# From the MLP's second tile on: all engines in the order of the text, weight sums spread over the second tile

## Chip, cores and metric

The kernel runs on one core of a Trainium2 chip. The metric is device time in microseconds (us) of one execution. A core has five engines with queues of their own: PE (TensorE, matmuls; PEld are its weight loads), DVE (VectorE), ACT (ScalarE), POOL (GpSimd) and SP (SyncE, which here issues nearly all DMAs). An engine works off its queue in order, and semaphores tie the queues together.

## The reference

Attention with a bias made of cumulative sums, then a Fourier mixing, then a normalised MLP with a residual:

```python
attn = softmax(causal(scale * q @ k.T + min(bias, 0))) @ v      # 8 batches, 8 heads, 576 x 64
x = attn.transpose(0, 2, 1, 3).reshape(8, 576, 512)
u = x + real(fft(fft(x, axis=1), axis=2))
un = (u - mean(u)) / sqrt(var(u) + 1e-6)
out = u + relu(un @ w_ch1) @ w_ch2                              # 512 -> 2048 -> 512
```

`w_ch1` and `w_ch2` come in double precision and are rounded to single in the kernel. Most matmul operands are split into a high part of fewer bits and a low remainder, and three matmuls replace one: high by high, low by high, high by low.

## The kernel before

Attention and Fourier mixing take about the first 680 us and leave `u` in DRAM, transposed: 512 channels in four blocks of 128 partitions, 4608 tokens along the free dimension. The MLP then runs over nine tiles of 512 tokens. The hidden dimension of 2048 is cut into 16 slices `f` of 128.

The first tile (`first_tile`, plain matmuls) shares its time with the end of the mixing and with the conversion of the weights out of double precision (`load_w`, `rounded`). The first layer's weights stay on chip as pairs (`wh`, `wl`). The second layer's go to DRAM (`wD`, line 120) and come back in each tile.

From the second tile on (`fast_tile`) two slices make a pair `g`, eight pairs in a tile. A pair's first layer is a 2 x 2 block product done with seven block products instead of eight (Strassen's scheme): seven products `k` of six matmuls each (line 338), whose results ACT and DVE combine in `cs` (lines 342 to 350), then relu on ACT (line 330, high part `zh`) and its remainder on DVE (line 331, `zl`). Three of the seven left operands are sums of weight blocks, made once by `sums_w(g)` (`sh`, `sl`: lines 144 to 164). The right operands are seven blocks of the tile's normalised tokens, four of them sums (`combine`, lines 230 to 233), split by `block` (lines 221 and 222).

Behind each product the text puts one or two groups of the second layer for the pair before: three matmuls (lines 249 to 251) into one of four accumulators. The weights of a slice's second layer are loaded by SP, cast on ACT, and the remainder is taken on POOL (`load_w2`, lines 127 to 129; four buffers). Both loads, casts and subtractions stand at the head of a pair; they are used in the pair after. When the last slice's group for a quarter `j` is through, in pair 0 of the next tile, `done(j)` multiplies the accumulator by the inverse deviation (DVE, line 276), adds `u` (POOL, line 277; `w`, fetched by line 275) and stores (SP, line 278). `o` and `w` have two buffers each.

Meanwhile `side(g, k)` prepares the next tile: `ln_tile` loads `u` (line 187), sums it (189 to 191), spreads the mean by a matmul with ones (68, 69, 177, 178), subtracts it (197), squares on ACT and adds on POOL in turn (200 to 203), takes the root and the reciprocal (208, 209); then `combine` and the blocks.

What sets the order: the text is traced once, and a planner with a cost model of its own orders each engine's queue. `tc.manual_schedule(engines={PE})` takes PE out of this from the second tile on: PE follows the order of the text, the other four are planned. The planner is free to draw later steps forward where it sees an engine idle.

Of the kernel before, what the change touches and what calls it, by code (L numbers as in the profile page):

```python
# [40 lines left out]
def fused_kernel(ctx, tc, qkT, vA, sP, wP, tabD, tabS, corr, out):  # L41
# [81 lines left out]
    def load_w2(f):  # L123

        h = w2p.tile([128, 512], F32R, tag="w2h", name="w2h", bufs=4)
        low = w2p.tile([128, 512], F32R, tag="w2l", name="w2l", bufs=4)
        nc.sync.dma_start(out=low.bitcast(F32), in_=wD[f, :, 512:1024])
        nc.scalar.copy(h, low.bitcast(F32))  # L128
        nc.gpsimd.tensor_sub(low, low.bitcast(F32), h.bitcast(F32))  # L129
        W2[f] = (h, low)  # L130

    def sums_w(g):

        (ah, al), (ch, cl) = W[2 * g], W[2 * g + 1]
        sh = sp.tile([128, 768], F32R, tag=f"sh{g}", name=f"sh{g}")
        sl = sp.tile([128, 768], F32R, tag=f"sl{g}", name=f"sl{g}")

        def tmp():
            return sx.tile([128, 256], F32, tag="sx", name="sx", bufs=5)

        def whole(h, low, x):
            t = tmp()
# [4 lines left out]
        def parts(t, h, low):  # L147
            nc.scalar.copy(h, t)
            nc.vector.tensor_sub(low, t, h.bitcast(F32))  # L149
# [5 lines left out]
        parts(a22, ch[:, 0:256], cl[:, 0:256])  # L155
        a11 = whole(ah, al, 0)
        s2 = tmp()
        nc.vector.tensor_sub(s2, a22, a11)
        parts(s2, sh[:, 0:256], sl[:, 0:256])
        yield 1.0  # L160
        nc.vector.tensor_sub(a21, a11, a21)
        parts(a21, sh[:, 256:512], sl[:, 256:512])
        a12 = whole(ah, al, 1)
        nc.vector.tensor_sub(a12, a12, s2)
        parts(a12, sh[:, 512:768], sl[:, 512:768])
        yield 1.0
        SW[g] = (sh, sl)

    W, W2, SW = {}, {}, {}

    def spread_sum(t, name):
# [3 lines left out]
        split(th, tl, t)  # L175
        m = bank(name)
        nc.tensor.matmul(m, ones, th, start=True, stop=False)
        nc.tensor.matmul(m, ones, tl, start=False, stop=True)
        return m

    def ltmp(name):
# [2 lines left out]
    def ln_tile(t0, lag):  # L184

        u = lnp.tile([128, 4, TOK], F32, tag="u", name="u")
        (nc.sync if t0 else nc.scalar).dma_start(out=u, in_=uD[:, :, t0:t0 + TOK].rearrange("c p t -> p c t"))
        t, t2 = ltmp("t"), ltmp("t2")
        nc.gpsimd.tensor_add(t, u[:, 0], u[:, 1])  # L189
        nc.vector.tensor_add(t2, u[:, 2], u[:, 3])  # L190
        nc.vector.tensor_add(t, t, t2)  # L191
        yield lag
        pm = spread_sum(t, "mu")
        mu = ltmp("mu")
        nc.scalar.copy(mu, pm)
        for j in range(4):
            nc.vector.tensor_sub(u[:, j], u[:, j], mu)
            yield 0.5
        t, t2 = ltmp("t"), ltmp("t2")
        nc.scalar.activation(t, u[:, 0], AF.Square)  # L200
        for j in range(1, 4):
            nc.scalar.activation(t2, u[:, j], AF.Square)
            nc.gpsimd.tensor_add(t, t, t2)  # L203
            yield 0.7
        yield lag
        pv = spread_sum(t, "var")
        r = lnp.tile([128, TOK], F32, tag="r", name="r", bufs=2)
        nc.scalar.activation(r, pv, AF.Sqrt, bias=eps)
        nc.vector.reciprocal(r, r)
        LN[t0] = (u, r)  # L210

    LN, BL = {}, {}

# [3 lines left out]
    def block(t0, k, src):  # L217

        h = bp.tile([128, 2, 256], F32R, tag="bh", name="bh", bufs=9)
        low = bp.tile([128, 2, 256], F32R, tag="bl", name="bl", bufs=9)  # L220
        nc.scalar.copy(h, src)
        nc.vector.tensor_sub(low, src, h.bitcast(F32))  # L222
        BL.setdefault(t0, {})[k] = (h, low)

    def combine(t0):
# [4 lines left out]
        nc.gpsimd.tensor_sub(t3, b22, b12)  # L230
        nc.vector.tensor_sub(b12, b12, b11)
        nc.vector.tensor_sub(t2, b22, b12)
        nc.vector.tensor_sub(t4, b21, t2)
        return [b11, b21, t2, b12, t3, b22, t4]

    held = []

# [20 lines left out]
    def accs():  # L258
        return [accp.tile([128, TOK], F32, tag=f"acc{j}", name=f"acc{j}") for j in range(4)]

    def writer(t0, acc, r):
        last = t0 + TOK == NT
        whole = []

        def done(j):
            if last and not whole:
                w = lnp.tile([128, 4, TOK], F32, tag="u", name="u")
                nc.sync.dma_start(out=w, in_=uD[:, :, t0:t0 + TOK].rearrange("c p t -> p c t"))
                whole.append(w)
            o = op.tile([128, TOK], F32, tag="o", name="o", bufs=2)  # L270
            if last:
                w = whole[0][:, j]
            else:
                w = op.tile([128, TOK], F32, tag="w", name="w", bufs=2)
                nc.sync.dma_start(out=w, in_=uD[j, :, t0:t0 + TOK])
            nc.vector.tensor_mul(o, r, acc[j])
            (nc.vector if last else nc.gpsimd).tensor_add(o, o, w)
            (nc.scalar if last and j % 2 else nc.sync).dma_start(out=out[j, :, t0:t0 + TOK], in_=o)

        return done  # L280

    def first_tile(t0):
        _, r = LN[t0]
        acc = accs()
        done = writer(t0, acc, r)
        bl = BL.pop(t0)
        load_w2(0)
        for f in range(NF):
            while min(f + 2, NF) not in W and next(feed, None) is not None:
                pass  # L290
            if f + 1 < NF:
                load_w2(f + 1)
            wh, wl = W[f]
            h = bank("h")
            for k in range(2):
                i = 0
                for a, b in ((wh, 0), (wl, 0), (wh, 1)):
                    for j in range(4):
                        nc.tensor.matmul(h[:, 256 * k:256 * k + 256], a[:, j * 128:(j + 1) * 128], bl[j // 2, k][b][:, j % 2], start=i == 0, stop=i == 11)
                        i += 1  # L300
            zh = zp.tile([128, TOK], F32R, tag="zh", name="zh", bufs=3)
            zl = zp.tile([128, TOK], F32R, tag="zl", name="zl", bufs=3)
            nc.scalar.activation(zh, h, AF.Relu)
            nc.vector.scalar_tensor_tensor(out=zl, in0=h, scalar=0.0, in1=zh.bitcast(F32), op0=ALU.max, op1=ALU.subtract)  # L304
            for g in groups():
                g()
            held.append((acc, zh, zl, f, done))
            yield 1.0

    def fast_tile(t0, side):  # L310
        _, r = LN[t0]
        bl = BL.pop(t0)
        acc = done = None
        for g in range(NF // 2):
            load_w2(2 * g)
            load_w2(2 * g + 1)
            todo = groups()
            n = len(todo)
            (ah, al), (ch, cl) = W[2 * g], W[2 * g + 1]
# [13 lines left out]
            for k, (p, start) in enumerate(((b1, True), (b2, True), (b1, False), (b3, True), (b1, False), (b3, False), (b1, False))):  # L333
# [22 lines left out]
                    relu(z[1], lo, p)  # L356
                for x in range(n * k // 7, n * (k + 1) // 7):
                    todo[x]()
                side(g, k)
            if g == 0:  # L360
                acc = accs()
                done = writer(t0, acc, r)
            held.extend((acc, z[x][0], z[x][1], 2 * g + x, done) for x in range(2))


# [361 lines left out]
    def plain(t0):  # L727
        for i in range(2):
            for k in range(2):
                block(t0, (i, k), quarter(LN[t0][0], i, k))  # L730
                yield 1.0

    stage_ctx = ExitStack()
# [89 lines left out]
    feed = rest()  # L823

    def early(t0):
        blocks.extend(combine(t0))
        for k in range(5):
            block(t0, k, blocks[k])
            yield 1.0

    blocks = []
    weave([first_tile(tiles[0]), NF], [chain(idle(1000), mixing), FOURIER * 0.6], [ahead(), 100],
          [later(chain(ln_tile(tiles[1], 1), early(tiles[1])), 4), 16])
    for _ in feed:
        pass
    for k in range(5, 7):
        block(tiles[1], k, blocks[k])
    for g in range(2):
        weave([sums_w(g), 1.0])
    order.enter_context(tc.manual_schedule(engines={mybir.EngineType.PE}))  # L840
    for x, t0 in enumerate(tiles[1:], 1):
        coming = tiles[x + 1] if x + 1 < len(tiles) else None
        norm = ln_tile(coming, 1) if coming is not None else iter(())
        blocks = []

        def side(g, k):
            if x == 1 and k % 2 == 0 and g + 2 < NF // 2:
                if k == 0:
                    adding[0] = sums_w(g + 2)
                next(adding[0], None)  # L850
            if coming is None:
                return
            if 1 <= g <= 5 and k % 3 == 2:
                next(norm, None)
            if g == 5 and k == 6:
                for _ in norm:
                    pass
                blocks.extend(combine(coming))
            if g == 6 and k in (2, 5):
                block(coming, k // 3, blocks[k // 3])  # L860
            if g == 7 and k < 5:
                block(coming, k + 2, blocks[k + 2])

        adding = [None]
        fast_tile(t0, side)
    for call_ in groups():
        call_()
    order.close()
# [138 lines left out]
```

## Time and profile before

| | us |
|---|---|
| median of 3 runs (1507.11 to 1510.95) | 1507.59 |
| the profiled execution | 1506.13 |
| its span, first to last instruction | 1504.4 |
| PE busy (88% of the span) | 1331.1 |
| DVE busy (61%) | 916.7 |
| ACT busy (48%) | 717.4 |
| POOL busy (46%) | 690.6 |

In rows of the timeline the columns are start and duration in us, engine, line of the kernel, operation, output<-inputs, shape and count; in brackets stands how long the engine sat idle before it and whose end released it. In the chain of work they are start, duration and what ran. In tables by stage, each engine's busy time and instruction count follow the stretch and its length; then come the granted TensorE clock, the share of DMA time and GB/s. A busy PE is not a PE at its peak, because matmuls overlap; the distance from one matmul's start to the next is the measure.

### The profile page before, as it was taken

What the parts mean: (1) busy time and instruction counts of PE and PEld (TensorE: products, weight loads), DVE (VectorE), ACT (ScalarE), POOL (GpSimd) and SP (SyncE); (2) the same over time, 40 slices, a digit from 0 to 9 for tenths busy, and PEclk for the clock granted to TensorE, in tenths of its full rate; (3) what the DMA queues carried; (4) which work ended last, traced back from release to release, by engine and by line L of the source; (5) the groups of instructions that cost most, each with busy time, mean ns of one, the idle gap of its engine ahead of it and who ended that gap; (6) DMA issues with size and microseconds to landing.
All of it is one profiled execution on the core that took longest, in us unless ns stands there. A gap on an engine that the chain in (4) does not pass through costs nothing.

```text
span 1504.4 us, 22206 instructions
## 1 busy us (share of the span) xinstructions
PE 1331.1 (88%) x7534; PEld 1126.7 (75%) x7534; DVE 916.7 (61%) x2034; ACT 717.4 (48%) x1641; POOL 690.6 (46%) x644
## 2 busy tenths in 40 slices
PE   4988979889898987777759999999999999999998
PEld 2766857677686766666548888888788888888897
DVE  6677677677767676969894453545536354453423
ACT  3776656666565653334434443434434344443432
POOL 6454546464546464655573252433425234252321
PEclk9998989999899988898879999999999999999999
DMA  8555655556555553424431231412313132231311
GB/s 212 155 156 156 153 152 137 165 140 176 159 160 152 135 157 123 137 75 149 141 126 56 77 100 49 134 49 71 105 50 127 50 109 67 66 110 50 120 50 56
DMA packets 106941, 173.50 MB, mean 115 GB/s; under 512 B 14408, under 2 KB 41897, under 8 KB 106827
## 3 DMA queue, kind: packets, MB, share of 16 engines
q1 hardware_dynamic: 104379, 168.08, 38.2%
q0 software_dynamic: 1632, 2.43, 0.8%
q10 hardware_dynamic: 816, 1.57, 0.3%
q8 instruction: 59, 0.97, 0.3%
q14 instruction: 55, 0.45, 0.1%
HBM read 122.39 MB, written 25.69 MB: 98 GB/s over the span
## 4 chain that ended last, share of the span: by engine, by line
PE 35%; DVE 5%; DMA 4%; POOL 4%; ACT 2%; issue 2%; SPq 0%; POOLq 0%; ACTq 0%; DVEq 0%
PE b L338 17%; PE acc L249 6%; PE acc L250 6%; PE acc L251 6%; DMA u<-uD 2%; POOL t L203 2%; DMA w2l<-wD 2%; POOL w2l L129 1%; DVE t L191 1%; POOL t L189 1%; ACT w2h L128 1%; DVE sl L149 0%; DVE bl L222 0%; DVE we L86 0%; DVE wm L84 0%
## 5 line engine op out<-in xcount | busy, mean ns | idle before, releaser
L129 POOL TENSOR_TENSOR w2l<-w2l,w2h 128x512 fp32r<-128x512 f32 x144 | 190.1, 1321 | 385.1 <-ACT w2h L128 334.1
L249 PE MATMUL acc<-zh,w2h 128*128 128x512 f32 x576 | 232.6, 404 | 19.5 <-ACT w2h L128 19.4
L250 PE MATMUL acc<-zh,w2l 128*128 128x512 f32 x576 | 232.8, 404 | 3.0 <-POOL w2l L129 2.9
L251 PE MATMUL acc<-zl,w2h 128*128 128x512 f32 x576 | 230.8, 401 | 4.0 <-DVE zl L304 4.0
L671 PE MATMUL pavB<-P,va 128*128 128x320 f32 (+2 forms) x640 | 199.2, 400 | 6.9 <-ACT stage L675 6.2
L643 ACT ACTIVATE P<-ps 128x320 f32<-128x320 f32 (+4 forms) x384 | 144.7, 391 | 114.7 <-PE ps L640 110.3
L607 PE MATMUL pm<-KQ 128*128 128x256 f32 (+4 forms) x384 | 158.1, 430 | 39.3 <-DVE Mx L614 19.3
L614 DVE CUSTOM_DVE_ANT_0 trash<-pm,amask 128x128 bf16<-128x128 f32 (+3 forms) x256 | 123.6, 483 | 79.3 <-PE pm L607 62.7
L639 PE MATMUL ps<-KQ 128*128 128x256 f32 (+3 forms) x384 | 152.7, 401 | 19.0 <-ACT P L643 12.2
L330 ACT ACTIVATE zh<-cs 128x256 fp32r<-128x256 f32 (+1 forms) x128 | 67.2, 525 | 162.0 <-DVE cs L350 98.6
L128 ACT CAST w2h<-w2l 128x512 fp32r<-128x512 f32 x144 | 88.8, 617 | 103.6 <-DMA w2l<-wD 103.1
L251 PEld LDWEIGHTS acc<-zl,w2h 128*128 128x128 f32 x576 | 110.9, 192 | 31.7 <-DVE zl L304 5.6
L249 PEld LDWEIGHTS acc<-zh,w2h 128*128 128x128 f32 x576 | 111.0, 193 | 26.7 <-ACT w2h L128 20.2
L671 PEld LDWEIGHTS pavB<-P,va 128*128 128x128 f32 (+1 forms) x640 | 106.4, 196 | 30.4 <-issue 12.4
L350 DVE TENSOR_TENSOR cs<-cs,b 128x256 f32<-128x256 f32 x64 | 26.9, 420 | 159.7 <-PE b L338 159.6
L640 PE MATMUL ps<-q,k 128*128 128x256 f32 (+3 forms) x384 | 119.8, 315 | 0.8 <-POOL q L586 0.8
L586 POOL TENSOR_TENSOR q<-qk,q 64x576 fp32r<-64x576 f32 x64 | 100.8, 1589 | 42.3 <-DMA q<-KQ 37.3
L607 PEld LDWEIGHTS pm<-KQ 128*128 128x128 f32 (+1 forms) x384 | 71.3, 188 | 64.4 <-DVE Mx L614 28.0
L338 PEld LDWEIGHTS b<-bh,wh 128*128 128x128 f32 x512 | 96.9, 190 | 29.8 <-DVE cs L350 7.2
L250 PEld LDWEIGHTS acc<-zh,w2l 128*128 128x128 f32 x576 | 111.0, 193 | 10.5 <-POOL w2l L129 5.4
L331 DVE SCALAR_TENSOR_TENSOR zl<-cs,zh 128x256 fp32r<-128x256 f32 (+1 forms) x128 | 72.5, 567 | 64.1 <-ACT zh L330 64.1
L338 PE MATMUL b<-bh,wh 128*128 128x256 f32 x512 | 102.9, 282 | 5.6 <-DVE cs L350 5.6
(171 smaller groups left out, 3089.6 us busy)
## 6 DMA issues: line engine op xcount, KB each, us to landing
w2l<-wD SPq DMA_DIRECT2D x144, 256.0 KB
qk<-in_qkT_dram SPq DMA_DIRECT2D x32, 576.0 KB
raw<-in_wP_dram SPq DMA_DIRECT2D x64, 256.0 KB
va<-in_vA_dram SPq DMA_DIRECT2D x32, 480.0 KB
q<-KQ SPq DMA_DIRECT2D x32, 288.0 KB
k<-KQ SPq DMA_DIRECT2D x32, 288.0 KB
rb<-rd SPq DMA_DIRECT2D x64, 144.0 KB
u<-uD SPq DMA_DIRECT2D x9, 1024.0 KB
```

The costliest lines, as they stand in the source:

```text
L128: nc.scalar.copy(h, low.bitcast(F32))
L129: nc.gpsimd.tensor_sub(low, low.bitcast(F32), h.bitcast(F32))
L249: nc.tensor.matmul(acc[j], a[:, cs], y, start=f == 0, stop=False)
L250: nc.tensor.matmul(acc[j], b[:, cs], y, start=False, stop=False)
L251: nc.tensor.matmul(acc[j], a[:, cs], z, start=False, stop=f == NF - 1)
L338: nc.tensor.matmul(p[:, 0:256], a[:, j * 128:(j + 1) * 128], b[:, j], start=start and i == 0, stop=i == 5, skip_group_check=not start)
L607: nc.tensor.matmul(p[:nq, :n], qy[:, h, 128 * c:128 * c + nq], ky[:, h, k0:k0 + n], start=True, stop=True)
L614: nc.vector.tensor_tensor_reduce(out=trash[:nq, :n], in0=p[:nq, :n], in1=amask[:nq, m0:m0 + n], scale=1.0, scalar=first if x else NEG, op0 ...
L639: nc.tensor.matmul(p[:nk, :n], ky[:, h, ksl], qy[:, h, a:a + n], start=True, stop=False)
L640: nc.tensor.matmul(p[:nk, :n], k1[:, h, ksl], q1[:, h, a:a + n], start=False, stop=True)
L643: nc.scalar.activation(P[:nk, o:o + a + n - lo], p[:nk, lo - a:n], AF.Exp, scale=0.125)
L671: nc.tensor.matmul(p[:, a - lo:n], va[:nk, c, vs], P[:nk, o:o + w], start=c == 0, stop=c == cs[-1])
```

## The change

From the second tile on the manual order holds for all engines (`tc.manual_schedule()`), and the steps that the planner placed so far get places in the text:

- `load_w2` is cut in two. The loads of a pair stand behind its first product, cast and subtraction (`split_w2`) behind the fourth product for the first slice and behind the fifth for the second.
- `sums_w` is cut in six steps, one behind each of a pair's first six products. Three remainder steps of 256 columns become one of 768, and the ACT casts likewise. As before, sums 0 and 1 are made ahead of the second tile and sums `g + 2` stand in the text of its pair `g`.
- `ln_tile` and `combine` are cut in 26 steps; `PLACES` lists the pair and product behind which each stands.
- A block's ACT cast and DVE subtraction are one product apart (`defer`, `tick`).
- `done` issues the multiplication; the add follows at the end of the same product, the store one product later, each time with the fetch of the next `w`. The first two `w` are fetched at the end of the tile before.
- In the first tile the next norm and the first blocks are woven in with other weights (18 for 16).

```diff
-        nc.scalar.copy(h, low.bitcast(F32))
-        nc.gpsimd.tensor_sub(low, low.bitcast(F32), h.bitcast(F32))
         W2[f] = (h, low)
+    def split_w2(f):
+        h, low = W2[f]
+        nc.scalar.copy(h, low.bitcast(F32))
+        nc.gpsimd.tensor_sub(low, low.bitcast(F32), h.bitcast(F32))
...
         a21 = whole(ch, cl, 0)
         a22 = whole(ch, cl, 1)
+        yield 1.0
         nc.vector.tensor_add(a22, a21, a22)
+        a11 = whole(ah, al, 0)
+        yield 1.0
+        nc.scalar.copy(ch[:, 0:256], a22)
+        nc.vector.tensor_sub(s[:, 0], a22, a11)
+        nc.vector.tensor_sub(s[:, 1], a11, a21)
+        a12 = whole(ah, al, 1)
+        yield 1.0
+        nc.vector.tensor_sub(cl[:, 0:256], a22, ch[:, 0:256].bitcast(F32))
+        nc.vector.tensor_sub(s[:, 2], a12, s[:, 0])
+        yield 1.0
+        f = s.rearrange("p a c -> p (a c)")
+        nc.scalar.copy(sh, f)
+        yield 1.0
+        nc.vector.tensor_sub(sl, f, sh.bitcast(F32))
...
+    def defer(n, call_):
+        soon.append([n, call_])
+    def tick():
+        now = [c for n, c in soon if n == 0]
+        soon[:] = [[n - 1, c] for n, c in soon if n]
+        for c in now:
+            c()
...
+            def add():
+                (nc.vector if last else nc.gpsimd).tensor_add(o, o, ws[j])
+            def store():
+                (nc.scalar if last and j % 2 else nc.sync).dma_start(out=out[j, :, t0:t0 + TOK], in_=o)
+                fetch()
+            if last:
+                add()
+                store()
+            else:
+                defer(0, add)
+                defer(1, store)
...
                 for x in range(n * k // 7, n * (k + 1) // 7):
                     todo[x]()
+                tick()
+                if k == 0:
+                    load_w2(2 * g)
+                    load_w2(2 * g + 1)
+                if k == 3 or k == 4:
+                    split_w2(2 * g + k - 3)
                 side(g, k)
...
-    order.enter_context(tc.manual_schedule(engines={mybir.EngineType.PE}))
+    order.enter_context(tc.manual_schedule())
+    PLACES = {(0, 1), (1, 1), (1, 3), (1, 4), (1, 5), (2, 0), (2, 1), (2, 2), (2, 3), (2, 4), (2, 5), *((3, k) for k in range(7)),
+              (4, 1), (4, 2), (4, 4), (4, 5), (5, 0), (5, 1), (5, 2), (5, 3)}
...
-            if x == 1 and k % 2 == 0 and g + 2 < NF // 2:
+            if x == 1 and g + 2 < NF // 2:
                 if k == 0:
                     adding[0] = sums_w(g + 2)
                 next(adding[0], None)
...
+            if (g, k) in PLACES:
+                next(norm)
...
+            if (g, k) in ((6, 2), (6, 5)):
+                defer(0, block(coming, k // 3, SRC[coming][k // 3]))
+            if g == 7 and 1 <= k <= 5:
+                defer(0, block(coming, k + 1, SRC[coming][k + 1]))
```

More of the change, by code (lines that the diff above doesn't have):

```diff
@@ L259, in accs, with fetch @@
         return [accp.tile([128, TOK], F32, tag=f"acc{j}", name=f"acc{j}") for j in range(4)]
+    soon = []
+    def defer(n, call_):
[5 more added lines that the diff above has]
+            c()
     def writer(t0, acc, r):
         last = t0 + TOK == NT
[L263 to L270, printed above, removed]
+        ws = []
+        def fetch():
+            j = len(ws)
+            if j == 4:
+                return
             if last:
-                w = whole[0][:, j]
+                if not ws:
+                    w = lnp.tile([128, 4, TOK], F32, tag="u", name="u")
+                    nc.sync.dma_start(out=w, in_=uD[:, :, t0:t0 + TOK].rearrange("c p t -> p c t"))
+                    ws.extend(w[:, x] for x in range(4))
             else:
@@ L275, in done @@
                 nc.sync.dma_start(out=w, in_=uD[j, :, t0:t0 + TOK])
+                ws.append(w)
+        def done(j):
+            o = op.tile([128, TOK], F32, tag="o", name="o", bufs=2)
             nc.vector.tensor_mul(o, r, acc[j])
-            (nc.vector if last else nc.gpsimd).tensor_add(o, o, w)
-            (nc.scalar if last and j % 2 else nc.sync).dma_start(out=out[j, :, t0:t0 + TOK], in_=o)
-        return done
+            def add():
[9 more added lines that the diff above has]
+                defer(1, store)
+        return fetch, done
     def first_tile(t0):
@@ L284, in first_tile @@
         acc = accs()
-        done = writer(t0, acc, r)
+        fetch, done = writer(t0, acc, r)
         bl = BL.pop(t0)
         load_w2(0)
+        split_w2(0)
         for f in range(NF):
@@ L308, in first_tile @@
             yield 1.0
+        fetch()
+        fetch()
     def fast_tile(t0, side):
@@ L361, in fast_tile @@
                 acc = accs()
-                done = writer(t0, acc, r)
+                fetch, done = writer(t0, acc, r)
+            if g == 7:
+                fetch()
+                fetch()
             held.extend((acc, z[x][0], z[x][1], 2 * g + x, done) for x in range(2))
@@ L825, in early @@
     def early(t0):
-        blocks.extend(combine(t0))
         for k in range(5):
-            block(t0, k, blocks[k])
-            yield 1.0
-    blocks = []
+            block(t0, k, SRC[t0][k])()
+            yield 0.5
     weave([first_tile(tiles[0]), NF], [chain(idle(1000), mixing), FOURIER * 0.6], [ahead(), 100],
-          [later(chain(ln_tile(tiles[1], 1), early(tiles[1])), 4), 16])
+          [later(chain(ln_tile(tiles[1], 1), combine(tiles[1]), early(tiles[1])), 4), 18])
     for _ in feed:
@@ L836, in fused_kernel @@
     for k in range(5, 7):
[L837 removed]
+        block(tiles[1], k, SRC[tiles[1]][k])()
     for g in range(2):
         weave([sums_w(g), 1.0])
[L840 removed]
+    order.enter_context(tc.manual_schedule())
+    PLACES = {(0, 1), (1, 1), (1, 3), (1, 4), (1, 5), (2, 0), (2, 1), (2, 2), (2, 3), (2, 4), (2, 5), *((3, k) for k in range(7)),
+              (4, 1), (4, 2), (4, 4), (4, 5), (5, 0), (5, 1), (5, 2), (5, 3)}
     for x, t0 in enumerate(tiles[1:], 1):
         coming = tiles[x + 1] if x + 1 < len(tiles) else None
[L843 to L844 removed]
+        norm = chain(ln_tile(coming, 1), combine(coming)) if coming is not None else iter(())
+        adding = [None]
         def side(g, k):
[L847 removed]
+            if x == 1 and g + 2 < NF // 2:
                 if k == 0:
@@ L852, in side @@
                 return
-            if 1 <= g <= 5 and k % 3 == 2:
-                next(norm, None)
-            if g == 5 and k == 6:
+            if (g, k) in PLACES:
+                next(norm)
+            if (g, k) == (5, 6):
                 for _ in norm:
                     pass
[L858 to L864, printed above, removed]
+            if (g, k) in ((6, 2), (6, 5)):
+                defer(0, block(coming, k // 3, SRC[coming][k // 3]))
+            if g == 7 and 1 <= k <= 5:
+                defer(0, block(coming, k + 1, SRC[coming][k + 1]))
         fast_tile(t0, side)
+    while soon:
+        tick()
     for call_ in groups():
```

57 lines of the change are left out of this document (28 added, 29 removed).

## The prediction

> **What bounds the kernel now.** I read the page first, then the engines' busy time by stage, then PE's waits, the chain that ended last, and the rows of the engines around single stalls.
>
> ```profile
> span 1504.4 us, 22206 instructions
> PE 1331.1 (88%) x7534; PEld 1126.7 (75%) x7534; DVE 916.7 (61%) x2034; ACT 717.4 (48%) x1641; POOL 690.6 (46%) x644
> ```
>
> ```profile
> 680.00:757.00 77.00, 55.87 (x271) 47.05 (x270) 71.20 (x154) 32.47 (x70) 42.98 (x45) 0.84 0.47 139
> 757.00:787.00 30.00, 13.30 (x54) 10.88 (x53) 29.78 (x43) 10.67 (x27) 22.20 (x21) 0.66 0.41 132
> 787.00:864.00 77.00, 73.93 (x458) 65.71 (x457) 35.77 (x60) 32.39 (x68) 24.74 (x18) 1.00 0.22 67
> ...
> 1407.00:1497.00 90.00, 89.57 (x552) 79.85 (x551) 26.89 (x56) 29.66 (x64) 26.06 (x20) 1.00 0.21 66
> ```
>
> The page averages stages with different limits, so the stages count (columns: PE, PEld, DVE, ACT, POOL busy, granted clock, DMA). In the first tile and the entry to the second (680 to 787) DVE is full: 71.2 of 77 us, then 29.8 of 30. From 787 on PE is the bound. In the last tile PE is busy all but 0.4 of 90 us; what the middle tiles lose follows below. The change touches both stages.
>
> How long should a tile take? The chain of one tile gives PE's pace:
>
> ```profile
> 860.01 5.15 DMA u<-uD
> ...
> 876.97 0.71 PE b L338 x6
> 877.92 0.23 PE acc L250
> ...
> 882.71 3.15 DMA w2l<-wD
> 885.94 0.63 ACT w2h L128
> 886.64 1.29 POOL w2l L129
> 887.96 1.69 POOL t L203
> 889.66 0.64 ACT t L202
> ...
> 894.59 0.28 ACT cs L346
> 894.91 0.97 PE b L338 x6
> ...
> 897.87 0.43 PE acc L249
> ```
>
> ```profile
> 894.91 0.50 PE L338 MATMUL b<-bh,sh 128*128 128x256 f32 x2 [2.38 <-ACT cs L346]
> 985.05 0.68 PE L338 MATMUL b<-bh,sh 128*128 128x256 f32 x2 [2.35 <-ACT cs L346]
> ```
>
> A product (six matmuls) takes 0.71, a group of three 3 x 0.23 = 0.70. A pair has seven products and eight groups: 10.57. Eight pairs and the norm's four matmuls make 8 x 10.57 + 4 x 0.23 = 85.5 us. The same stall comes again after 985.05 - 894.91 = 90.1, so a middle tile loses 4.7. Half of it is this stall: ACT's queue holds the copy that PE waits for behind a norm that alternates between POOL and ACT, and the chain starts in a late load of w2 (882.71). The rest is small waits and a stretch in which a matmul takes 0.43 for 0.23.
>
> **Part by part: the entry.** Today:
>
> ```profile
> 757.24 0.32 SPq L120 DMA_DIRECT2D wD<-we  x1
> 760.94 1.27 SPq L127 DMA_DIRECT2D w2l<-wD  x3
> ```
>
> ```profile
> 768.10 0.62 ACT L68 CAST th<-t 128x512 fp32r<-128x512 f32 x1 [3.21 <-DVE t L191]
> ...
> 768.93 0.61 ACT L128 CAST w2h<-w2l 128x512 fp32r<-128x512 f32 x1
> ```
>
> ```profile
> 769.59 0.80 PE L249 MATMUL acc<-zh,w2h 128*128 128x512 f32 x1 [11.88 <-ACT w2h L128]
> ...
> 782.88 0.51 PE L338 MATMUL b<-bh,wh 128*128 128x256 f32 x2 [4.25 <-DVE cs L350]
> ...
> 787.35 0.40 PE L338 MATMUL b<-bh,wh 128*128 128x256 f32 x2
> ```
>
> DVE's share that belongs to the weight sums (all instructions on their temporaries):
>
> ```profile
> 680.00:757.00 77.00, 12.64 (x20) 3.99 (x10) 7.58 (x9) 0.84 0.47 139
> 757.00:790.00 33.00, 21.62 (x29) 5.65 (x15) 10.83 (x12) 0.69 0.43 139
> ```
>
> Eight sets are 64 DVE instructions today; 35 run before 757, because the planner draws all sets forward. Afterwards only two sets (16 of today's size) can precede the second tile, and by their number they fit ahead of 680. So up to 12.6 us leave a stage where DVE is the bound. I take 8, since other chains of that stage become visible, with bounds 3 and 12. The last w2 rows then remain: written at 757.24, loaded at 760.94, landed 3.2 later (882.71 to 885.94), cast 0.6, so PE could go on at 764.8 instead of 769.59. The cast stands behind the next norm's `th`, which the text now puts a pair later: another -4.8. The second tile's first pair (769.59 to 787.35, 17.8 us) holds the 4.25 wait and slow matmuls; its five remaining products and four groups are 6.4 at full pace and about 10.5 with the first 7 us at the slow one: -7. Entry: -20 (-12 to -25).
>
> **The second tile** now makes six sets in pairs 0 to 5. DVE and POOL block each other:
>
> ```profile
> 866.99 1.28 POOL L129 TENSOR_TENSOR w2l<-w2l,w2h 128x512 fp32r<-128x512 f32 x1
> 867.07 1.75 DVE L191 TENSOR_TENSOR t<-t,t 128x512 f32<-128x512 f32 x1 [1.19 <-POOL t L189]
> ```
>
> ```profile
> 874.12 0.68 DVE L331 SCALAR_TENSOR_TENSOR zl<-cs,zh 128x512 fp32r<-128x512 f32 x1
> 874.72 0.42 DVE L331 SCALAR_TENSOR_TENSOR zl<-b,zh 128x256 fp32r<-128x256 f32 x1
> ```
>
> A DVE instruction of 512 elements takes 0.68 alone and 1.75 when it meets POOL: it ends 0.55 after POOL does. So their times add. A set has four POOL adds (10.83/12 = 0.9 each), five DVE steps of 0.42 and one of 768, an estimate of 0.95 from 0.42 and 0.68. That is 6.6, and with two w2 subtractions (2.6) and the two relu remainders from SBUF (1.1) it fills a pair of 10.57. The output adds in pair 0 (5), the norm in pairs 1, 2, 3 and the combination in pair 5 (2 to 4 each) come on top: 13 to 16 us of excess. Today the tile's seven other pairs keep PE busy 73.9 of 77. I take +12 (+4 to +20).
>
> **Each middle tile.** The norm's squares get places of their own, so the 2.4 us stall goes. What is late next is w2 of pair 1:
>
> ```profile
> 870.17 0.68 DVE L276 TENSOR_TENSOR o<-r,acc 128x512 f32<-128x512 f32 x1
> ...
> 878.11 0.69 DVE L276 TENSOR_TENSOR o<-r,acc 128x512 f32<-128x512 f32 x1 [0.94 <-DMA out_dram<-o]
> ```
>
> ```profile
> 875.97 0.34 SPq L278 DMA_DIRECT2D out_dram<-o  x1
> 876.36 0.43 SPq L275 DMA_DIRECT2D w<-uD  x1
> 876.88 0.40 SPq L127 DMA_DIRECT2D w2l<-wD  x1
> ```
>
> ```profile
> 879.75 1.30 POOL L277 TENSOR_TENSOR o<-o,w 128x512 f32<-128x512 f32 x1 [1.21 <-DMA w<-uD]
> ```
>
> ```profile
> 880.29 0.62 ACT L128 CAST w2h<-w2l 128x512 fp32r<-128x512 f32 x1 [3.60 <-DMA w2l<-wD]
> ```
>
> Today pair 1's first load leaves SP at 876.88, ahead of two output stores. In the new text both loads follow the fourth store. Its chain: first `mul` as now at 870.2, done 870.9; POOL takes the add and two w2 subtractions (3 x 1.3), 874.8; the second `mul`, held behind a relu remainder that meets the last subtraction, ends 875.9; its add 877.2, store 877.3. The fourth `mul` needs that store's buffer: 2.1 to land (875.97 to 878.11). The fourth add needs `w`, issued behind the store and 3.3 under way (876.36 to 879.7): 881.0 to 882.3. So the loads leave at 882.7, land at 885.9. ACT meets the cast in the fourth product of pair 1, about 880, and holds everything behind it: relu, second cast, `th`, then the 512-wide relu, which also waits for two DVE steps behind the first relu: about 888.5 to 889.1, if it takes the 0.63 of the cast at 885.94. Pair 1 starts at 874.8 without stalls, so pair 2's first group wants that relu at 874.8 + 10.57 + 0.71 = 886.1: 3.1 late; its remainder adds 0.3, the mean's matmuls 0.4: 3.8. Part of it appears earlier, at pair 1's last product, since DVE's add of `t` waits for POOL behind the fourth add. Bounds: 2.5 when the remainder misses the subtraction, 5 when one more meets. Behind the fourth `mul` DVE holds pair 1's first addition until about 880; nobody wants that bank for another two products. Slow matmuls: the 2.38 idle at 894.91 brought about 3.3 us at 0.43 for 0.23, 1.5 lost; the new idle comes in two parts, so I take 0.9. Squares behind two subtractions on POOL: 0.3. Sum 5.0 against 4.7: +0.3 a tile, six tiles +2. The ends are 2.5 + 0.3 and 5 + 1.5 + 0.3 a tile, so -11 to +13 for six.
>
> On the slow matmuls a rule differs from the row at 894.91. The Trainium skill (TensorE: Matmul & The Clock Gate, Why this matters for your kernels) says that gaps under some 3 us keep the matmuls at full rate; by it the 0.9 would be nothing, about 6 us less in all. The trace disagrees, since 2.38 us sufficed.
>
> **The last tile** has the same store chain and loses almost nothing today: +4 (0 to +5). At nothing I cost the blocks' deferred subtractions, the reciprocal, the fetches of `w` moved into the tile before, and the load of `u`, which moves past two w2 loads on SP into pair 0: it takes 5.15 (860.01) and is wanted a pair, 10.57, later. PE's products cover them; uncovered, a DVE step costs its 0.7 and the load 5.
>
> Sum: -20 + 12 + 2 + 4 = -2. The profiled execution took 1506.13 (span 1504.4 and 1.7 around it), 1.5 under the median 1507.59. So I forecast 1505 against that median.
>
> **The rivals.** (1) Faster: ACT isn't held, because stores land early enough or the late relus still meet their groups. Then a middle tile loses about 1.5, as little as the last tile suggests is possible: -3.2 x 6 = -19, the last 0, the entry -20, the second tile +12: 1480. For it: the big stall has one cause, which the new places remove. Against: the late load already starts today's chain at 882.71, and the text doesn't bring it forward. (2) Slower: the exclusion of DVE and POOL decides. It sits in the second tile's pairs 0 to 5, costs 20 there, and 1.5 in each middle tile, where DVE's remainders meet w2 subtractions at fixed places (+9); last tile +5, entry -15: 1527. It decides from the point where a pair's shared time exceeds 10.57 us; above I count that in five pairs of the second tile. The Trainium skill (SBUF — State Buffer, SBUF: two separate sides) states such an exclusive lock; the 1.75 at 867.07 agrees. (3) The change doesn't do what it says: the planner still mixes the text's order with the first tile's work and draws sums forward. Entry -5, second tile 0, the rest +6: 1509.
>
> **How the numbers follow.** Forecast 0.42 (1496 to 1512), faster rival 0.25, slower 0.27, third 0.06. About 0.3% (4.5 us) is what a measurement of this kernel can tell from no change: 1503.1 to 1512.1. Of the forecast's 0.42, 0.15 lies below and 0.22 inside, 0.05 above goes with the slower. With the third's 0.05 inside: faster 0.40, within 0.27, slower 0.33. The range goes into both rivals: 1482 to 1523.
>
> **What would show it.** Right: no DVE instruction of sums 2 to 7 ahead of the second tile; PE's 11.88 wait under 5; in middle tiles ACT waiting 4 to 6 us for `w2l<-wD` in pair 1, and PE's stall at pair 2's first group, released by `zh` or `zl`. Wrong: middle tiles at 87 us or less (rival 1); a second tile over 100 us (rival 2); sums still before 757 (rival 3).

## The result and the profile after

The changed kernel took 1491.07 us (median; 1487.01 to 1492.89) beside 1507.35 for the kernel before on the same chip: a ratio of 0.9884 (0.9858 to 0.9909), some 16 us faster. The forecast was 1505, with 0.40 on faster. The profiled execution took 1487.01, of which the span is 1485.3. The page after, engines' busy time:

```profile
span 1485.3 us, 22158 instructions
PE 1321.9 (89%) x7534; PEld 1120.4 (75%) x7534; DVE 893.4 (60%) x2018; ACT 703.1 (47%) x1625; POOL 688.4 (46%) x644
```

Busy time hardly says where 19 us of span went: PE has the same 7534 matmuls and 9 us less, DVE 23 us less of work that is mostly off the path. The stages say more. The kernel after, busy time by stage (columns as in the prediction):

```profile
680.00:740.00 60.00, 43.81 (x228) 37.43 (x228) 57.74 (x121) 24.06 (x50) 27.53 (x31) 0.89 0.54 163
...
757.00:787.00 30.00, 25.14 (x137) 21.21 (x136) 21.73 (x35) 10.04 (x23) 19.67 (x18) 0.89 0.26 78
...
849.00:937.00 88.00, 86.19 (x534) 76.39 (x533) 40.95 (x72) 36.02 (x79) 34.11 (x25) 1.00 0.27 84
```

In 757 to 787, where PE had 13.3 us of work before, it has 25.1; DVE, full there before, has 21.7 of 30. A middle tile (849 to 937) keeps PE busy for 86.2 of 88 us.

To compare kernels I cut the trace by PE's own work: a tile has 336 product matmuls, so a tile runs from its first product to the next tile's first. The entry runs from the first tile's first MLP matmul to PE's first second-layer group in the second tile, and the second tile is counted from that group.

| us | before | after | difference | forecast |
|---|---|---|---|---|
| entry | 180.3 | 166.1 | -14.3 | -12.8 |
| second tile, pair 0 | 15.3 | 10.8 | -4.5 | -7 |
| second tile, pairs 1 to 7 | 79.4 | 87.9 | +8.5 | +12 |
| six middle tiles | 542.6 | 535.7 | -6.8 | +2 |
| last tile, to the end | 97.6 | 100.6 | +3.0 | +4 |
| sum | 915.2 | 901.0 | -14.1 | -2 |

The other 5.0 us between the two profiled executions lie ahead of the first MLP matmul (589.3 before, 584.3 after), where the change only cuts the first tile's norm finer. In the seven kernels below whose text is the changed one's up to there (all but POOL in order and the last two), that point lay anywhere from 587.4 to 593.0, so the 5.0 isn't put down to the change.

**The entry.** The kernel after, instructions on the weight sums' temporaries (DVE, ACT, POOL):

```profile
680.00:740.00 60.00, 0.00 (x0) 0.00 (x0) 0.00 (x0) 0.89 0.54 163
760.00:850.00 90.00, 16.61 (x25) 2.04 (x5) 19.37 (x20) 0.94 0.20 61
```

Before, 20 DVE instructions of sums (12.64 us) ran from 680 to 757. Now none runs from 680 to 740: those of sums 0 and 1 run ahead of 680, and the rest begin behind PE's first second-layer group, in the second tile. The kernel after, SP's queue, then ACT's, then PE's around the first second-layer group:

```profile
740.60 4.36 SPq L120 DMA_DIRECT2D wD<-we  x2
746.59 0.32 SPq L127 DMA_DIRECT2D w2l<-wD  x1
749.66 0.62 ACT L133 CAST w2h<-w2l 128x512 fp32r<-128x512 f32 x1 [6.33 <-DMA w2l<-wD]
750.33 0.80 PE L265 MATMUL acc<-zh,w2h 128*128 128x512 f32 x1 [4.23 <-ACT w2h L133]
```

PE's wait of 11.88 is 4.23 now. The cast starts 3.1 us after its load was issued, behind nothing else on ACT.

**The middle tiles.** PE's waits in the six middle tiles, before and then after (total, times, longest, in us):

```profile
PE b L338 <- ACT cs L346: 17.0, 11, 3.1
```

```profile
PE acc L265 <- ACT zh L376: 10.1, 6, 3.3
PE b L384 <- DVE cs L396: 4.4, 6, 1.7
```

The releaser has changed as forecast: not the copy into `cs` behind the norm, but pair 2's first group, which waits for the relu `zh`. The kernel after, SP's queue, then ACT's, then PE's in the middle tile that starts at 849.0:

```profile
861.33 0.34 SPq L314 DMA_DIRECT2D out_dram<-o  x1
861.72 0.42 SPq L303 DMA_DIRECT2D w<-uD  x1
862.58 4.01 SPq L314 DMA_DIRECT2D out_dram<-o  x2
866.69 4.40 SPq L127 DMA_DIRECT2D w2l<-wD  x4
```

```profile
869.61 0.62 ACT L133 CAST w2h<-w2l 128x512 fp32r<-128x512 f32 x1 [4.61 <-DMA w2l<-wD]
...
872.30 0.63 ACT L376 ACTIVATE zh<-cs 128x512 fp32r<-128x512 f32 x1 [0.23 <-DVE cs L399]
```

```profile
868.60 0.39 PE L384 MATMUL b<-bh,wh 128*128 128x256 f32 x1 [0.50 <-DVE cs L396]
...
872.98 0.50 PE L265 MATMUL acc<-zh,w2h 128*128 128x512 f32 x1 [1.31 <-ACT zh L376]
```

Read from top to bottom: SP stands at the second of two output stores, whose add POOL ends at 866.23, until the w2 load leaves at 866.69, 17.7 us after the tile's start; ACT sits 4.61 in front of its cast; the 512-wide relu starts at 23.3; PE waits 1.31 for it. That is the forecast chain, each step 0.7 to 1.0 us earlier than forecast (18.4, 21.6, 24.2).

### The profile page after: what moved, and what is told of

It is laid out like the page before. It is cut to its first block, busy times and chain, and to the rows that moved or that the text cites. A ratio compares the mean times of both kernels' runs of the same rounds, so it can differ in the third digit from the quotient of the medians.

```text
span 1485.3 us, 22158 instructions
## 1 busy us (share of the span) xinstructions
PE 1321.9 (89%) x7534; PEld 1120.4 (75%) x7534; DVE 893.4 (60%) x2018; ACT 703.1 (47%) x1625; POOL 688.4 (46%) x644
## 4 chain that ended last, share of the span: by engine, by line
PE 39%; DVE 10%; DMA 6%; POOL 4%; issue 2%; ACT 2%; SPq 0%; POOLq 0%; DVEq 0%; ACTq 0%
PE b L384 18%; PE acc L265 7%; PE acc L267 7%; PE acc L266 7%; DMA w2l<-wD 2%; DVE wm L87 1%; DVE we L82 1%; DVE we L86 1%; POOL o L311 1%; ACT zh L376 1%; DMA w<-uD 1%; DVE wm L84 1%; POOL t L213 1%; POOL w2l L134 1%; DMA raw<-in_wP_dram 1%
## 5 line engine op out<-in xcount | busy, mean ns | idle before, releaser
L134 POOL TENSOR_TENSOR w2l<-w2l,w2h 128x512 fp32r<-128x512 f32 x144 | 199.2, 1386 | 339.7 <-ACT w2h L133 336.8
L694 PE MATMUL ps<-KQ 128*128 128x256 f32 (+3 forms) x384 | 152.6, 400 | 23.3 <-ACT P L698 14.6
L377 DVE SCALAR_TENSOR_TENSOR zl<-cs,zh 128x256 fp32r<-128x256 f32 (+1 forms) x128 | 88.5, 691 | 95.5 <-ACT zh L376 95.5
L726 PEld LDWEIGHTS pavB<-P,va 128*128 128x128 f32 (+1 forms) x640 | 104.8, 194 | 31.2 <-issue 12.2
L694 PEld LDWEIGHTS ps<-KQ 128*128 128x128 f32 (+1 forms) x384 | 72.1, 188 | 49.9 <-ACT P L698 21.9
```

Source lines behind the costliest of these rows:

```text
L694: nc.tensor.matmul(p[:nk, :n], ky[:, h, ksl], qy[:, h, a:a + n], start=True, stop=False)
L726: nc.tensor.matmul(p[:, a - lo:n], va[:nk, c, vs], P[:nk, o:o + w], start=c == 0, stop=c == cs[-1])
```

## The experiments

The theory after the result: the cut steps and the sums' places shorten the entry and the middle tiles, and what a middle tile still loses comes from the w2 loads behind the stores. The rivals: the text's order on all engines brings the gain, not the cuts; and the entry is quicker for another reason than the sums. All results in one table (us, stages from the profiled execution, ratio to the kernel before as it was timed beside each, with its 95% interval):

| kernel | ratio | median | entry | second tile | middle tiles, mean | last |
|---|---|---|---|---|---|---|
| before | | 1507.35 | 180.3 | 94.7 | 90.4 | 97.6 |
| after | 0.9884 (0.9858 to 0.9909) | 1491.07 | 166.1 | 98.7 | 89.3 | 100.6 |
| loads first | 0.9849 (0.9814 to 0.9884) | 1482.21 | 166.8 | 98.5 | 88.1 | 96.9 |
| sums ahead | 0.9917 (0.9892 to 0.9943) | 1493.54 | 178.3 | 87.8 | 88.5 | 102.2 |
| planner | 0.9942 (0.9921 to 0.9962) | 1497.76 | 183.2 | 93.5 | 88.8 | 98.5 |
| before, POOL in order | 1.0066 (1.0039 to 1.0093) | 1516.64 | 162.4 | 113.8 | 91.2 | 97.6 |
| loads first, late norm | 0.9748 (0.9721 to 0.9776) | 1470.38 | 168.6 | 96.9 | 86.1 | 97.1 |
| late norm alone | 0.9994 (0.9971 to 1.0017) | 1507.43 | 167.3 | 96.6 | 91.3 | 101.1 |
| sums on DVE | 0.9831 (0.9807 to 0.9856) | 1482.62 | 163.4 | 95.6 | 88.7 | 100.9 |
| all three | 0.9699 (0.9659 to 0.9738) | 1461.89 | 163.2 | 94.4 | 86.1 | 96.9 |
| + reciprocal later | 0.9682 (0.9658 to 0.9707) | 1458.20 | 161.9 | 90.4 | 86.2 | 96.9 |
| + second sum early | 0.9644 (0.9619 to 0.9669) | 1452.80 | 160.3 | 90.6 | 85.2 | 96.9 |

### The w2 loads ahead of the stores

```diff
-                tick()
                 if k == 0:
                     load_w2(2 * g)
                     load_w2(2 * g + 1)
+                tick()
```

> The changed kernel with one thing turned round: behind a pair's first product both w2 loads are issued before the output steps that are due there (the third and fourth store in pair 1). Theory (SP's order holds ACT): the loads leave at the head of pair 1, about 11 us after the tile's start instead of 17.7, land by 15, and ACT's cast no longer waits; PE's wait of some 1.5 to 3 us at pair 2's first group goes, and the slow matmuls behind it. A middle tile falls from 89.3 us on average to 86 to 87, the last tile loses 3 us, in all 18 to 22 us off the changed kernel: about 1470. Rival (the norm on POOL and DVE is what holds pair 1): the wait at pair 2 stays over 1 us and the whole moves by less than 5 us.

Measured: the last tile loses 3.7 of its 100.6 us, the middle tiles 1.2 each. Pair 2 of a middle tile falls from 13.0 to 11.0, so the stall at its first group is gone, and it was the loads' place that made it. But pair 1 rises from 11.3 to between 12.4 and 15.5. Loads first, one middle tile (start 854.3): POOL, DVE, PE.

```profile
870.63 1.29 POOL L311 TENSOR_TENSOR o<-o,w 128x512 f32<-128x512 f32 x1 [2.73 <-DMA w<-uD]
871.88 1.29 POOL L195 TENSOR_TENSOR t<-u 128x512 f32<-128x512 f32 x1
873.13 1.27 POOL L134 TENSOR_TENSOR w2l<-w2l,w2h 128x512 fp32r<-128x512 f32 x1
```

```profile
873.21 1.74 DVE L198 TENSOR_TENSOR t<-t,t 128x512 f32<-128x512 f32 x1 [2.80 <-POOL t L195]
874.87 0.41 DVE L396 TENSOR_TENSOR cs<-cs,b 128x256 f32<-128x256 f32 x1
```

```profile
875.33 0.38 PE L384 MATMUL b<-bh,wh 128*128 128x256 f32 x1 [1.91 <-DVE cs L396]
```

The last `w` is issued as early in the tile as before but comes 0.5 us later, with the loads now under way beside it (POOL waits 2.73 for it, 2.25 in the changed kernel). Behind the add comes the norm's own add on POOL; DVE waits 2.80 for that in order, then takes 1.74 beside a POOL subtraction that now comes early enough to meet it (0.69 in the changed kernel), and `cs`, which PE needs, stands behind it. Of the 1.5 us by which `cs` comes later in its tile than in the changed kernel, 0.4 came with the late `w` and 1.0 is this slower step. One wait has taken the place of another: not quite half of the theory's gain came (8.9 us of 18 to 22).

### All eight sums ahead of the manual order

```diff
-    for g in range(2):
+    for g in range(NF // 2):
         weave([sums_w(g), 1.0])
...
-            if x == 1 and g + 2 < NF // 2:
+            if x == 0 and g + 2 < NF // 2:
```

> The changed kernel, but all eight sets of weight sums stand ahead of the second tile in the text, where the planner may place them. Theory (the entry's gain is the six sets that left a full DVE): PE's first group of the second tile goes back from 750.3 to 764 or later, and the second tile, without sums, takes 88 us from that group on instead of 98.7; net 2 to 10 us slower than the changed kernel, 1493 to 1500. Rival (the entry's gain comes from the text order itself, which keeps the next norm behind the last w2 cast): the first group stays under 757 and the kernel gets some 8 us faster than the changed one.

Measured: the entry is 178.3, 12.3 longer than the changed kernel's, and the second tile 87.8, 10.8 shorter. Sums ahead, ACT, then PE, at the first group:

```profile
768.18 0.41 ACT L155 CAST wh<-sx 128x256 fp32r<-128x256 f32 x1 [0.72 <-DVE sx L152]
769.11 0.62 ACT L133 CAST w2h<-w2l 128x512 fp32r<-128x512 f32 x1 [0.53 <-DMA w2l<-wD]
```

```profile
769.78 0.80 PE L265 MATMUL acc<-zh,w2h 128*128 128x512 f32 x1 [4.82 <-ACT w2h L133]
```

The first group is back at 769.78. What moves is the last first-layer matmul: it comes 170.5 us after the first one, in the changed kernel 157.9. From it to the first group the time stays as in the changed kernel (7.9 and 8.2; 15.3 in the kernel before), though a cast of the sums stands just ahead. So the sums' place sets the first part of the entry; the second part is shortened by the order of the text, as the rival had it. Moving the sums is worth 12.3 in the entry for 10.8 given back: nearly nothing by itself (the medians are 2.5 apart, and the intervals overlap).

### The text after, but only PE in its order

```diff
-    order.enter_context(tc.manual_schedule())
+    order.enter_context(tc.manual_schedule(engines={mybir.EngineType.PE}))
```

> The changed kernel's text, with all its cuts and places, but only PE in manual order, as before. Theory (the order counts, not the cuts): the planner draws the sums forward again, the first group comes at 764 or later, a middle tile takes 89 to 91 us, the whole 1503 to 1512. Rival (the cuts alone do it, with fewer and longer DVE steps): under 1495.

Measured 1497.76; neither side had this. The entry is 183.2, as the theory said: the planner draws the sums forward, as the rows on their temporaries show (planner):

```profile
680.00:740.00 60.00, 8.31 (x11) 1.22 (x3) 6.72 (x8) 0.82 0.46 140
```

But the middle tiles take 88.8, where the expectation was no better than 89. PE's waits there (planner):

```profile
PE acc L265 <- ACT zh L376: 6.3, 6, 1.1
PE b L384 <- ACT cs L394: 4.1, 4, 1.0
PE b L384 <- ACT cs L392: 2.2, 8, 0.5
```

All are about 1 us or less, against 3.1 before. So the cut and newly placed steps, with the planner still free, take 10.0 us out of the six middle tiles. The manual order then gives 17.2 in the entry and takes back 5.2 in the second tile, 3.1 in the middle ones and 2.1 in the last: 6.8 net, as the medians say (6.7).

### The text before, with POOL in its order too

```diff
-    order.enter_context(tc.manual_schedule(engines={mybir.EngineType.PE}))
+    order.enter_context(tc.manual_schedule(engines={mybir.EngineType.PE, mybir.EngineType.Pool}))
```

> The kernel before, with POOL besides PE in the order of the text. POOL's adds begin each weight sum, so sums 2 to 7 can't be drawn ahead of the second tile; DVE, ACT and SP stay with the planner. Theory (the entry's gain is the sums): first group of the second tile between 750 and 757, second tile longer by 3 to 12 us from there, middle tiles 89 to 92 us: 1492 to 1502. Rival (the sums don't hold the entry): first group at 766 or later, no gain.

Missed: slower than before, 1516.64. The entry came as expected (162.4), so holding POOL's steps in place is enough for it (the next norm's adds are held along with the sums'). But the second tile then takes 113.8. PE's waits in it (POOL in order, second tile):

```profile
PE b L338 <- ACT cs L348: 9.4, 5, 2.4
PE acc L251 <- DVE zl L331: 4.5, 2, 2.5
```

A second tile in which the sums stay whole at their place is 19 us longer than before; the changed kernel's, with sums in steps, is 4 longer. So the entry's gain was lost again here. That it is the cuts that save it in the changed kernel is argued and not shown, since the two differ in the other engines' order as well.

### The norm later, with and without the loads first

All the norm's steps from its first adds to its squares stand later. Those behind pair 1's second and fourth products move behind its fifth and seventh, those behind its fifth and sixth into pair 2, and the steps after them by one or two products:

```diff
-    PLACES = {(0, 1), (1, 1), (1, 3), (1, 4), (1, 5), (2, 0), (2, 1), (2, 2), (2, 3), (2, 4), (2, 5), *((3, k) for k in range(7)),
-              (4, 1), (4, 2), (4, 4), (4, 5), (5, 0), (5, 1), (5, 2), (5, 3)}
+    PLACES = {(0, 1), (1, 4), (1, 6), *((2, k) for k in range(7)), *((3, k) for k in range(7)), (4, 0),
+              (4, 1), (4, 2), (4, 4), (4, 5), (5, 0), (5, 1), (5, 2), (5, 3)}
```

> Both w2 loads ahead of the output steps, as in e1_loads_first, and the next norm's steps two to eighteen stand later: first sums behind pair 1's fifth product, DVE's add of t behind the seventh, cast, remainder and mean in pair 2. Theory (in e1 what was late next was DVE's add of t: it waits for POOL behind the fourth output add, and the addition that frees PE's bank stands behind it): pair 1 falls from 12.4 to 15.5 us in e1 to 10.6 or 11.0, no pair of a middle tile over 11.5, a middle tile at 86.0 to 86.5 instead of 88.1; 9 to 13 us off e1, about 1470. Rival (the late output adds themselves hold pair 1): pair 1 stays at 12 us or more and the gain over e1 is under 4 us.

> The changed kernel with the later norm steps of e5 and nothing else, so the w2 loads still follow the fourth store. Theory (two waits in a row, of which the later, ACT's on the load, sets the time): pair 1 falls from 11.3 to 10.6, pair 2 takes back what pair 1 gives, 13.3 to 13.8 where it was 13.0, and a middle tile stays within 1 us of the changed kernel's 89.3. Rival (the waits are separate): the middle tile falls by the 0.8 of pair 1 and more, to 87 or less.

With the loads first: 1470.38, middle tiles 86.1, pair 1 at its bare 10.55. As the theory said. Without them: 1507.43, nothing of the changed kernel's gain left, which neither theory had. (By stages the middle tiles take back 12.2 us in all; in this profile the rest lies ahead of the first MLP matmul, where the two texts are alike.) Pair 1 runs at 10.55 there too, but pair 2 takes 15.6 to 17.8. Late norm alone, one middle tile (start 856.9): ACT, DVE, POOL.

```profile
878.54 0.62 ACT L133 CAST w2h<-w2l 128x512 fp32r<-128x512 f32 x1 [5.59 <-DMA w2l<-wD]
...
882.88 0.63 ACT L376 ACTIVATE zh<-cs 128x512 fp32r<-128x512 f32 x1 [2.88 <-DVE cs L399]
```

```profile
879.51 1.27 DVE L377 SCALAR_TENSOR_TENSOR zl<-cs,zh 128x256 fp32r<-128x256 f32 x1 [5.04 <-ACT zh L376]
880.71 1.74 DVE L196 TENSOR_TENSOR t<-u 128x512 f32<-128x512 f32 x1
882.38 0.41 DVE L399 TENSOR_TENSOR cs<-cs,b 128x256 f32<-128x256 f32 x1
```

```profile
879.24 2.66 POOL L134 TENSOR_TENSOR w2l<-w2l,w2h 128x512 fp32r<-128x512 f32 x2 [5.14 <-ACT w2h L133]
```

In the changed kernel this norm step on DVE (line 196) ran at 864.40, before ACT came to its cast. Moved later, it falls behind the relu that follows the cast: DVE has idled 5.04, and now two of its steps in a row meet POOL's subtractions (1.27 and 1.74). The add that the 512-wide relu needs is done only at 882.8, so the relu starts 26.0 us after the tile's start instead of 23.3, and PE pays that and its slow matmuls. Of these 2.7 us 1.0 is the cast, which starts later in this tile (21.6 for 20.6), and 1.7 the step in between.

### The sums' adds on DVE instead of POOL

```diff
-            nc.gpsimd.tensor_add(t, h[:, xs].bitcast(F32), low[:, xs].bitcast(F32))
+            nc.vector.tensor_add(t, h[:, xs].bitcast(F32), low[:, xs].bitcast(F32))
```

> The changed kernel with the four adds of each weight sum on DVE instead of POOL. Theory (in the second tile the two engines' exclusion and the wait for each other in order cost the time, not DVE's own work): 1.7 us more of DVE work a pair, 3.6 us less on POOL; the second tile from its first group falls from 98.7 to 93 to 96 us. Rival (DVE's own work is the bound there): 99 us or more.

As expected: the second tile falls from 98.7 to 95.6 though DVE has more to do. The changed kernel, second tile, pair 1 (start 761.13): POOL, then DVE, then PE.

```profile
763.25 3.15 POOL L311 TENSOR_TENSOR o<-o,w 128x512 f32<-128x512 f32 x2 [1.34 <-DVE o L308]
766.36 2.12 POOL L146 TENSOR_TENSOR sx<-wh,wl 128x256 f32<-128x256 f32 x3
768.43 1.45 POOL L195 TENSOR_TENSOR t<-u 128x512 f32<-128x512 f32 x1
```

```profile
767.81 0.94 DVE L152 TENSOR_TENSOR sx<-sx 128x256 f32<-128x256 f32 x1 [2.57 <-POOL sx L146]
768.68 1.75 DVE L196 TENSOR_TENSOR t<-u 128x512 f32<-128x512 f32 x1
```

```profile
774.51 0.80 PE L384 MATMUL b<-bh,wh 128*128 128x256 f32 x2 [3.32 <-DVE cs L396]
```

Two costs of the POOL adds show. They stand behind the output adds on POOL and DVE waits 2.57 for them; and DVE is slow beside POOL: 0.94 for a step of 256 columns next to the last of these adds (0.42 alone), and 1.75 for one of 512 (0.69 alone) next to the norm's own add, which has slid behind them. With the adds on DVE, pair 1 is 13.1 instead of 17.4; which of the two costs weighs more isn't separated. Pair 5 gets worse (16.7 for 15.0): DVE's own time is what counts there. The Trainium skill (SBUF — State Buffer, SBUF: two separate sides) has the second cost as an exclusive lock of ports; these rows and this run agree with it.

### The three together, and two more steps

> Loads ahead of the output steps, later norm steps and the sums' adds on DVE together. Theory: the gains add, middle tiles at 86.0 to 86.5 us, second tile at 92 to 96 from its first group: 1465 to 1470. Rival (the second tile's waits are of one chain with the norm's steps): no better than e5_late_norm by more than 2 us.

The loads first, the norm later and the sums on DVE give 1461.89, better than forecast. The gains add up: 20.7 for the first two together and 8.5 for the third, taken from 1491.07, leave 1461.9. Two waits stand out in what is left (all three, from the second tile's first group to the end):

```profile
PE b L384 <- DVE cs L396: 4.0, 2, 3.2
PE acc L265 <- ACT zh L376: 2.6, 5, 0.9
```

The first is for the most part the second tile's pair 5 (3.2), where DVE makes the reciprocal (line 219; the row is from the kernel after, the step is the same):

```profile
814.83 3.33 DVE L219 RECIPROCAL r<-r 128x512 f32<-128x512 f32 x1
```

`r` is first wanted in the tile after, so the reciprocal can stand behind `combine`, in pair 6:

```diff
-        nc.vector.reciprocal(r, r)
+    def invert(t0):
+        _, r = LN[t0]
+        nc.vector.reciprocal(r, r)
...
-        norm = chain(ln_tile(coming, 1), combine(coming)) if coming is not None else iter(())
+        norm = chain(ln_tile(coming, 1), combine(coming), invert(coming)) if coming is not None else iter(())
```

> e8_all_three with the reciprocal of the next norm (3.3 us on DVE) moved from the head of pair 5 behind pair 6's first product, after the combination. Theory (in the second tile's pair 5 DVE's own time is over the pair, since a set of sums meets the reciprocal and the combination there): the second tile's pair 5 falls from 15.7 to 11 to 12.5 us, middle tiles stay at 86.1: 3 to 4 us off e8, about 1458. Rival (the combination on POOL and DVE is what fills the pair): pair 5 stays over 14 us.

Pair 5 falls from 15.7 to 11.6, the second tile from 94.4 to 90.4. The other wait comes from the norm's DVE sum `t2` in front of the addition to `cs` that the relu needs (all three, DVE in a middle tile):

```profile
864.99 1.78 DVE L196 TENSOR_TENSOR t<-u 128x512 f32<-128x512 f32 x1
```

It needs only `u`, so it can go to pair 1's second product, into time in which DVE idles, and POOL's `t` stays late:

```diff
-        nc.gpsimd.tensor_add(t, u[:, 0], u[:, 1])
         nc.vector.tensor_add(t2, u[:, 2], u[:, 3])
+        yield 0.0
+        nc.gpsimd.tensor_add(t, u[:, 0], u[:, 1])
```

> e9_reciprocal_later with one DVE step of the next norm (the sum of the third and fourth quarter) back at pair 1's second product, where DVE is idle; its partner on POOL stays behind the fifth. Theory (this step meets POOL's w2 subtractions, takes 1.7 us in place of 0.7 and holds the addition in front of the 512-wide relu): the wait at pair 2's first group, 0.5 to 0.9 us with slow matmuls behind it, goes; pair 2 falls from 11.5 to 12.2 us to 11.0 to 11.2, a middle tile from 86.1 to 85.1 to 85.5, 4 to 6 us off e9. Rival (the late casts of w2 alone make that relu late): pair 2 stays at 11.5 us or more.

1452.80, the best of all: 53.8 us under the kernel before as timed beside it (1506.61). Second sum early, busy time in one middle tile:

```profile
839.80:925.00 85.20, 85.20 (x534) 76.56 (x533) 41.61 (x72) 36.01 (x79) 34.74 (x25) 1.00 0.28 87
```

PE waits for nothing in any of the six. 85.2 is what a tile takes without losses; the prediction worked out 85.5.

## Why the prediction was right and wrong

The time lies inside the range given (1482 to 1523), and each stage inside the bounds that the working gave it. It lies outside the 1496 to 1512 of the forecast itself.

**The entry** was right in kind and nearly in size. The last first-layer matmul comes 7.1 earlier (forecast 8), and from there to the first group it is 7.2 less (forecast 4.8). For the first part, sums ahead and POOL in order show the cause from both sides: with all the sums drawn forward that matmul comes 170.5 us after the first one, with POOL held to the order even in the old text 154.3; in the kernel before it is 165.0. The second part doesn't hang on the sums, since it stays short with them ahead. It has two pieces. The cast starts 3.1 us after its load's issue and not 8.0, no longer behind the next norm's `th`: 4.9 for the 4.8 forecast. And the load leaves SP 2.3 sooner behind that matmul, which the working didn't have. With the planner back in charge `th` stands ahead of the cast again (769.46 and 769.98), and the part grows to 11.0. The term for **pair 0** was taken from a wrong row: 787.35 is pair 1's second product, so the pair took 15.3 before and not 17.8. Its new length (10.8) was forecast as 10.5, hence -4.5 and not -7. By luck this and the 7.2 nearly cancel.

**The second tile** costs +8.5, not the +12 taken, inside the 4 to 20 given. That POOL's adds cost time there is shown, for pair 1, by the run with the adds on DVE. The working had 13 to 16 us of excess, less some 3 that PE idles there today (73.9 busy of 77). The excess is there: pairs 1 to 7 take 87.9, and in a middle tile without losses 74.7, 13.2 less. But it doesn't lie on every one of pairs 0 to 5. It stands mostly in two, pair 1 (17.4) and pair 5 (15.0, with the reciprocal in it); the five pairs between and behind them take 10.6 to 11.9. The mis-sized term is the loss of the kernel before in these pairs, 4.7 (79.4 against 74.7): besides the idle time it holds slow matmuls at the head of pair 1 (0.43 apart for 0.23), which count as busy. So 13.2 - 4.7 makes the 8.5.

**The middle tiles** hold most of the gap between 1505 and 1491: -6.8 instead of +2. The step that failed is the sum "5.0 against 4.7". The chain itself is in the trace, step by step, and loads first shows that it is the cause of pair 2's stall. Its sizes were off, each a little. PE's wait was put at 3.8. Three of the six tiles lose 2.75 (0.76 in pair 1, 2.0 in pair 2), because the remainder in front of the second `mul` wasn't held, as the working had it: it took 0.69 and the subtraction beside it 1.82 for 1.29, so POOL paid for that meeting and not DVE; the other three wait longer, by 0.9, 2.0 and 1.4, which makes 3.45 on the mean. Slow matmuls cost 1.3 and 2.1 in two tiles, 0.6 on the mean, for the 0.9. The squares' 0.3 doesn't exist. Together that is 4.1, not 5.0. And the kernel before loses 5.2 on the mean of six against a bare tile of 85.2, where one distance between two stalls and 85.5 had given 4.7. Six times 0.9 + 0.5 is 8.4 of the gap of 8.8. The stall did change its place as forecast, but the new one is smaller than the old, not larger.

What the prediction missed in kind is what the planner run shows: the cut and placed steps help the planner as well, by 10.0 us in the middle tiles, more than the manual order keeps of it. The text's order for all engines earns its time in the entry alone.

**The faster rival** came nearest in time (1480) and was wrong in its reason: ACT is held in every middle tile, 4.5 to 6.3 us. With the loads ahead alone its time isn't reached (1482.21); with the norm later as well it is passed (1470.38). **The slower rival** needed a second tile over 100; it took 98.7. **The third** fell: none of sums 2 to 7 runs ahead. **The last tile** was right: +3.0 for +4, and the loads in front of the stores take all of it away.

Two points stay open. How much of the 19 us in the second tile of the POOL-in-order kernel is waiting and how much is DVE and POOL slowing each other wasn't separated. A third buffer for `o` and `w`, which might free the stores' chain without moving the loads, wasn't tried.

## What to carry to other kernels

In a queue that follows the text, a transfer's place is a decision about everything behind it: a load issued behind a store that waits holds an engine several steps away, and moving it ahead can bring another wait to light, so go on until the waits are gone and not until the first one is. A step that runs in the idle time of a stalled chain costs nothing there, and moved "out of the way" it can land inside the chain, where it costs whatever the gain was (late norm alone). Try the cut and placed steps with the free planner before giving up the planner: the new text and the order are two changes with separate prices.

## What the hardware showed

The granted clock can drop after waits of PE that are not long. PE's timeline at three waits, in the kernel after, the kernel before and sums on DVE, and then PE's busy time, granted clock and DMA behind each of the three, in the same order:

```profile
1049.77 0.50 PE L265 MATMUL acc<-zh,w2h 128*128 128x512 f32 x1 [2.23 <-ACT zh L376]
...
1075.23 0.50 PE L338 MATMUL b<-bh,sh 128*128 128x256 f32 x2 [2.35 <-ACT cs L346]
...
1224.90 0.50 PE L265 MATMUL acc<-zh,w2h 128*128 128x512 f32 x1 [1.55 <-ACT zh L376]
```

```profile
1051.70:1053.70 2.00, 2.00 (x10) 0.51 0.04 8
...
1075.20:1077.20 2.00, 1.97 (x13) 1.00 0.00 0
...
1226.90:1228.90 2.00, 2.00 (x9) 0.50 0.00 0
```

Behind 2.23 and 1.55 PE goes on at half of the full clock, behind 2.35 at full clock; the waits of 1.31 and 1.74 in the kernel after were followed by full clock too (1.00). So in these runs the length of a wait alone doesn't decide, and what does stays open. A stall that brings the drop has two prices: the tile with the 2.23 is 2.2 us longer than the undisturbed ones, of which only 0.9 is the longer wait. The Trainium skill (TensorE: Matmul & The Clock Gate, Why this matters for your kernels) puts the limit at about 3 us without matmuls; here 2.23 and 1.55 sufficed, as 2.38 did before the change.

On DVE, a reciprocal of 512 columns took 3.33 to 3.35 in the kernel after, with POOL at work beside it or not, an addition of the same size 0.69 alone. In a queue where PE waits for additions, it is worth a place of its own (the second tile's 4.0 us above).
